# Attention and gated network on one core: stores of the folded weights put ahead in their queues, and other banks for the first transposes

## Chip, core and metric

The kernel runs on one core of a Trainium2 chip. The metric is the device time of one execution in microseconds (us). TensorE (PE) multiplies, VectorE (DVE), ScalarE (ACT) and GpSimd (POOL) work elementwise, SyncE (SP) issues most of the DMAs. Each engine takes its own instructions in the order of its queue and waits on semaphores for those of others.

## What is computed

Four batches of eight heads, 768 positions, 64 columns a head: attention over a window of 15 positions to each side and over 24 block summaries (the maximum of the keys and the mean of the values of each block of 32). The result, 3072 tokens by 512, goes through a gated network.

```python
k_sum = k.reshape(B, H, nb, block, D).max(axis=3)
v_sum = v.reshape(B, H, nb, block, D).mean(axis=3)
scores_all = concat([where(mask_l, scale * q @ k.T, -1e9), scale * q @ k_sum.T + log(block)])
a = softmax(scores_all)
x = (a @ concat([v, v_sum])).transpose(0, 2, 1, 3).reshape(B * S, H * D)
a = x @ w1
b = x @ w2
out = (a * b @ w3) @ w_out
```

## The kernel before

**Folding.** `w3 @ w_out` is multiplied once, at the start, into eight tiles `wp0` to `wp7` of 128 by 512 (in the trace's order their names are wp_80 to wp_87). Every weight arrives in halves as raw words (`wraw`), is rebuilt on ACT (L167) and DVE (L175, L178), cast on ACT into a high part (L188) and subtracted on DVE into a low part (L109). Products take three passes: high by high, low by high, high by low. `fold_weights` (from L193) accumulates tile i over j = 0 to 7 in one PSUM bank. When j = 7 is done, `store` (L209) empties the bank: a cast on ACT (L211, `wp`), and a subtraction on DVE (L109, `wp`) that needs the cast. The bank is free only after both.

**Banks.** PSUM has eight. Two carry the tag `mm` (products of the network, and fold tiles 0, 1 and 4 to 7), two the tag `tp` (transposes, the attention's output `po`, and the fold tiles 2 and 3, by `SIDE` = 4, L199), four the tag `sc` (scores, and the product of the means). A tile takes the next bank of its tag in turn.

**Attention in steps.** A step s is a pair of heads for 512 tokens. On PE it has scores (`sc`, L319, 32 small matmuls), transposes of the softmax (`tp`, L373, 16) and the product with the values (`po`, L393, 32). In between, DVE subtracts the maximum (L333, eight), ACT takes exponentials (L347, eight, each with its sum), POOL and DVE invert the sum (L352, L353), and ACT normalises (L362, eight; in step 0 it is one DVE instruction, L364). ACT copies the transposes out (L378 and L380 or, by `SECOND`, DVE for the second); after `po` ACT casts and DVE subtracts into `x` (L404, L109).

**Order.** PE and SP run in the order written. In the first stage the loop over `t` (L641) interleaves the fold, the conversions of weights and the first eight steps (`first_pair`, L555), which begin at the times of `FIRST`. ACT, DVE and POOL are ordered by a scheduler's priorities, which follow the order of the program; `tc.high_priority(offset=SOONER)`, with 400, moves instructions ahead of up to that much earlier work. The network's own evacuations have it already (L434, L437, L456). Later stages take two steps at a time, with the second step's transposes in `sc` banks.

Of the kernel before, what the change touches and what calls it, by code (L numbers as in the profile page):

```python
# [48 lines left out]
SECOND = "AAAVAVVA"  # L49
SOONER = 400  # L50
# [20 lines left out]
def attention_moe(ctx, tc, qG, kW, kT, vP, vW, vB, mask, w1, w2, w3T, wo, out):  # L71
    nc = tc.nc
# [33 lines left out]
    wp = [const.tile([P, 2, DO], F32R, name=f"wp{i}") for i in range(NF)]  # L106

    def low(eng, dst, src, hi):
        eng.tensor_tensor(dst, src, hi.bitcast(F32), ALU.subtract)  # L109

    def products(acc, terms, first, last):
        for i, (a, b) in enumerate(terms):
            nc.tensor.matmul(acc, lhsT=a, rhs=b, start=first and i == 0, stop=last and i == len(terms) - 1)  # L113
# [79 lines left out]
    def fold_weights(order):  # L193
        acc = {}
        for i, j in order:
            while not {("w3", i, j * P // PIECE), ("wo", j // 2, j % 2 * DO // PIECE)} <= have:
                yield 0
            if j == 0:
                acc[i] = ps.tile([P, 512], F32, name="mm", tag="tp" if 2 <= i < SIDE else "mm", bufs=2)  # L199
            a, b = weights["w3", i][:, :, j], weights["wo", j // 2][:, :, j % 2]  # L200
            products(
                acc[i][:, :DO],
                [(a[:, 0], b[:, 0]), (a[:, 1], b[:, 0]), (a[:, 0], b[:, 1])],
                j == 0,
                j == NJ - 1,
            )
            yield 3 * DO

            def store(i=i):  # L209
                done = acc.pop(i)[:, :DO]  # L210
                nc.scalar.copy(wp[i][:, 0], done)  # L211
                low(nc.vector, wp[i][:, 1], done, wp[i][:, 0])

            if j == NJ - 1:
                later(store)
# [112 lines left out]
    def reduce(u, h, sc, sm, mx):  # L328

        for i in ORDER:  # L330
            blk = (u * NBLK + i) % BLOCKS
            j = h * NBLK + i
            nc.vector.tensor_tensor_reduce(  # L333
                out=sm[:, j],
                in0=sc[h][:, i * KR : (i + 1) * KR],
                in1=mask_sb[:, 0 if blk == 0 else 2 if blk == BLOCKS - 1 else 1],
                op0=ALU.add,
                op1=ALU.min,
                scale=-SCALE,
                scalar=3.0e38,  # L340
                accum_out=mx[:, 0, j : j + 1],
            )

    def expose(h, sm, mx):
        for i in ORDER:
            j = h * NBLK + i
            nc.scalar.activation(  # L347
                sm[:, j], sm[:, j], AF.Exp, bias=mx[:, 0, j : j + 1], scale=-1.0, accum_out=mx[:, 1, j : j + 1]
            )

    def invert(mx):
        nc.gpsimd.tensor_scalar(out=mx[:, 1], in0=mx[:, 1], scalar1=1e-9, scalar2=None, op0=ALU.add)  # L352
        nc.vector.reciprocal(mx[:, 2], mx[:, 1])  # L353

    def normalize(sm, mx):
        nc.gpsimd.tensor_tensor(sm, sm, mx[:, 2].unsqueeze(2).broadcast_to([P, NI, KR]), ALU.mult)  # L356

    def normalize_alone(s, sm, mx):

        if NORMALIZE[s] == "A":  # L360
            for j in range(NI):
                nc.scalar.activation(sm[:, j], sm[:, j], AF.Copy, scale=mx[:, 2, j : j + 1])  # L362
        else:
            nc.vector.tensor_tensor(sm, sm, mx[:, 2].unsqueeze(2).broadcast_to([P, NI, KR]), ALU.mult)  # L364

    def transposes(sm, **more):

        tp = [ps.tile([P, 512], F32, name="tp", **more or {"bufs": 2}) for _ in range(2)]
        for j in range(NI):
            for g in range(2):  # L370
                rows = slice(64 * g, 64 * g + 64)
                to, p = tp[g][:KR, j * 64 : j * 64 + 64], sm[rows, j]
                nc.tensor.transpose(to, p, ident[rows, rows])  # L373
        return tp

    def evacuate(tp, second="V"):
        pt = [sb.tile([KR, U], F32, name="pt", bufs=6) for _ in range(2)]
        nc.scalar.copy(pt[0], tp[0][:KR, :U])  # L378
        if second == "A":
            nc.scalar.copy(pt[1], tp[1][:KR, :U])  # L380
        else:
            nc.vector.tensor_copy(pt[1], tp[1][:KR, :U])  # L382
        return pt

    def outputs(pt, v):

        po = ps.tile([P, 512], F32, name="po", tag="tp", bufs=2)
        for i in range(NBLK):
            for g in range(2):
                at = (2 * i + g) * 64  # L390
                for h in range(2):
                    cols = slice(h * D, (h + 1) * D)
                    nc.tensor.matmul(  # L393
                        po[cols, at : at + 64],
                        lhsT=v[:, g, i, cols],
                        rhs=pt[g][:, (h * NBLK + i) * 64 : (h * NBLK + i + 1) * 64],
                        start=True,
                        stop=True,
                    )
        return po  # L400

    def keep_x(po, x):
        t = sb.tile([P, 2, U], F32R, name="x", bufs=6)
        nc.scalar.copy(t[:, 0], po[:, :U])  # L404
        low(nc.vector, t[:, 1], po[:, :U], t[:, 0])
        x.append(t)
# [99 lines left out]
    def place(s):  # L506
        return divmod(s, NPAIR)

    inputs, values, sms = {}, {}, {}

    def fetch(s):
        if s < NS:
            inputs[s] = load_scores(*place(s))

    def fetch_values(s):
        if s < NS:
            values[s] = load_values(*place(s))

    def fetch_sums(s):
        if s < NS:  # L520
            load_sums(*place(s), values[s])

    def fill(s):
        if s < NS:
            gather(*place(s), inputs[s][1])

    def begin(s):
        u, p = place(s)
        sm = sb.tile([P, NI, KR], F32, name="sm", tag="wf", bufs=5)
        mx = aligned([P, 3, NI], name="mx", bufs=4)  # L530
        sms[s] = sm, mx
        return u, sm, mx, scores(*inputs.pop(s))
# [14 lines left out]
    def prepare(s):  # L547
        for work, raw in loaded.pop(s, ()):
            work(raw)
        for load_, work in coming.pop(s, ()):  # L550
            loaded.setdefault(s + 1, []).append((work, load_()))
# [3 lines left out]
    def first_pair(s):  # L555

        u, sm, mx, sc = begin(s)
        yield
        reduce(u, 0, sc, sm, mx)
        reduce(u, 1, sc, sm, mx)  # L560
        expose(0, sm, mx)
        yield
        expose(1, sm, mx)
        invert(mx)
        yield
        normalize_alone(s, sm, mx)
        while t[0] < (FIRST + (FIRST[-1] + 5,))[s + 1]:
            yield
        pt = evacuate(transposes(sms.pop(s)[0]), SECOND[s])
        yield  # L570
        keep_x(outputs(pt, values.pop(s)), xs[u])

# [2 lines left out]
    def later(work):  # L575
        delayed.append([1, work])
# [106 lines left out]
    with tc.manual_schedule(engines={engines.PE}):  # L683
        for s in range(NFIRST, NS + 1, 2):
            now = (s, s + 1) if s < NS else ()
            last = (s - 2, s - 1) if s > NFIRST else ()
            for p in (s, s + 1):
                prepare(p)
                if s == NFIRST:
                    fetch(p)  # L690
                    fill(p)
                    fetch_values(p)
                    fetch_sums(p)
            for p in (s + 2, s + 3):
                fetch(p)
                fetch_values(p)
                fetch_sums(p)
            with tc.manual_schedule(engines={engines.Activation, engines.DVE}):
                spare = ({}, {"tag": "sc", "bufs": 4})
                tps = [transposes(sms.pop(p)[0], **more) for p, more in zip(last, spare)]  # L700
                pts = [evacuate(tp) for tp in tps]
                begun_now = [begin(p) for p in now]
                for p, pt in zip(last, pts):
                    keep_x(outputs(pt, values.pop(p)), xs[place(p)[0]])
                for u, sm, mx, sc in begun_now:
                    for h in range(2):
                        reduce(u, h, sc, sm, mx)
                        expose(h, sm, mx)
                    invert(mx)
                    normalize(sm, mx)  # L710
            for p in (s + 2, s + 3):
                fill(p)

            n = s + 2 - NFIRST
            m = NPAIR + 0.15
            run(ALL_FOLD + UNIT * (1 + (n / m if n <= m else 1 + (n - m) / NPAIR)))
        run(float("inf"))
# [57 lines left out]
```

## Time and profile before

| | us |
|---|---|
| median of three runs | 540.87 (540.83 to 541.28) |
| the profiled execution | 540.83 |
| its span in the trace | 539.0 |
| PE busy | 517.9 (96%) |
| DVE busy, ACT busy | 237.5, 238.9 (44% each) |
| POOL busy | 56.3 (10%) |

The profiled execution is 1.8 us longer than its span. Shares of the whole span hide that the first 130 us, with folding, conversion of weights and attention at once, are full on all engines, and that the rest is almost PE alone. In 40 slices of 13.5 us:

```profile
PE   2897999999999999999999999999999999999997
PEclk9988899999999999999999999999999999999999
DMA  8999689956524005544032141050160020000001
```

### The profile page before, as it was taken

How to read it: one execution, taken by the hardware profiler on the slowest of the kernel's cores; microseconds unless marked ns; L12 is line 12 of the kernel's file. 1: busy time of each engine (PE TensorE's matmuls, PEld its weight loads, DVE VectorE, ACT ScalarE, POOL GpSimd, SP SyncE). 2: the span in 40 equal slices, each digit the busy share in tenths (PEclk: the TensorE clock that was granted, in tenths of full speed). 3: DMA queues.
4: the chain of work that ended last, by engine and by line, in shares of the span. 5: the costliest groups of instructions: out<-in, count | busy, mean ns of one | idle time of the engine just before them, and what ended most of it. 6: DMA issues, size and time to landing. Idle time of an engine off the chain costs nothing.

```text
span 539.0 us, 9912 instructions
## 1 busy us (share of the span) xinstructions
PE 517.9 (96%) x3852; PEld 421.8 (78%) x3852; DVE 237.5 (44%) x686; ACT 238.9 (44%) x688; POOL 56.3 (10%) x103
## 2 busy tenths in 40 slices
PE   2897999999999999999999999999999999999997
PEld 1655777888788888888888888888888888888885
DVE  5868889999503226724244033252042351122210
ACT  5547898887345225226235144253162261222210
POOL 1001221111001101103003002011021020000000
PEclk9988899999999999999999999999999999999999
DMA  8999689956524005544032141050160020000001
GB/s 309 403 348 350 189 270 369 280 183 197 167 96 154 0 1 169 162 128 135 0 111 60 40 152 58 0 157 33 40 190 1 1 75 39 21 21 0 1 19 58
DMA packets 30574, 67.21 MB, mean 125 GB/s; under 512 B 4032, under 2 KB 7616, under 8 KB 30528
## 3 DMA queue, kind: packets, MB, share of 16 engines
q1 hardware_dynamic: 27072, 60.30, 35.2%
q10 hardware_dynamic: 3456, 6.29, 3.1%
q8 instruction: 30, 0.49, 0.4%
q14 instruction: 16, 0.13, 0.1%
HBM read 58.51 MB, written 6.29 MB: 120 GB/s over the span
## 4 chain that ended last, share of the span: by engine, by line
PE 91%; DVE 3%; ACT 3%; DMA 1%; issue 1%; POOL 0%; SPq 0%; POOLq 0%; ACTq 0%
PE mm L113 79%; PE po L393 5%; PE sc L319 4%; PE tp L373 2%; DVE w L109 1%; DMA wraw<-in_w3T_dram 1%; DVE wf L178 1%; ACT w L188 1%; PE means L260 1%; ACT sm L347 1%; DVE wf L175 1%; ACT wf L167 0%; ACT wp L211 0%; DVE wp L109 0%; POOL k L306 0%
## 5 line engine op out<-in xcount | busy, mean ns | idle before, releaser
L113 PE MATMUL mm<-x,w 128*128 128x512 f32 x1152 | 264.9, 390 | 0.0
L113 PEld LDWEIGHTS mm<-x,w 128*128 128x128 f32 x1152 | 215.4, 188 | 45.6 <-issue 0.5
L113 PE MATMUL mm<-wp,h 128*128 128x512 f32 x576 | 133.9, 391 | 0.0
L113 PEld LDWEIGHTS mm<-wp,h 128*128 128x128 f32 x576 | 107.5, 188 | 22.7 <-issue 0.2
L347 ACT ACTIVATE sm<-sm,mx 128x120 f32<-128x120 f32 x192 | 73.6, 387 | 19.9 <-DVE mx L333 19.9
L438 DVE TENSOR_TENSOR g<-mm,g 128x512 f32<-128x512 f32 x48 | 33.1, 689 | 90.6 <-PE mm L113 88.7
L439 ACT CAST h<-g 128x512 fp32r<-128x512 f32 x48 | 29.6, 618 | 87.7 <-DVE g L438 87.7
L113 PE MATMUL mm<-w,w 128*128 128x512 f32 x192 | 54.1, 435 | 12.6 <-ACT w L188 11.5
L113 PEld LDWEIGHTS mm<-w,w 128*128 128x128 f32 x192 | 38.2, 206 | 25.6 <-ACT w L188 13.3
L457 ACT COPY o<-mm 128x512 f32<-128x512 f32 x24 | 14.1, 585 | 81.3 <-PE mm L113 81.3
L109 DVE TENSOR_TENSOR h<-g,h 128x512 fp32r<-128x512 f32 x48 | 35.7, 743 | 24.2 <-ACT h L439 24.0
L435 ACT COPY g<-mm 128x512 f32<-128x512 f32 x48 | 28.0, 584 | 35.6 <-PE mm L113 35.2
L333 DVE CUSTOM_DVE_ANT_0 sm<-sc,mask_sb 128x120 f32<-128x120 f32 x192 | 41.0, 275 | 5.5 <-PE sc L319 5.5
L382 DVE COPY pt<-tp 120x512 f32<-120x512 f32 x19 | 12.4, 686 | 67.7 <-PE tp L373 67.7
L306 POOL COPY k<-ks 128x96 f32<-128x96 f32 (+1 forms) x32 | 10.1, 327 | 252.3 <-DMA k<-in_kW_dram 210.0
L347 ACT ACTIVATION_READ_ACCUMULATOR sm<-sm,mx 128x1 f32 x192 | 36.5, 190 | 0.0
L109 DVE TENSOR_TENSOR x<-po,x 128x512 fp32r<-128x512 f32 x24 | 16.6, 690 | 42.2 <-ACT x L404 42.2
L356 POOL TENSOR_TENSOR sm<-sm,mx 128x960 f32<-128x960 f32 x16 | 29.1, 1820 | 6.0 <-DVE mx L353 5.0
L167 ACT ACTIVATE wf<-wraw 128x512 f32<-128x512 f32 x40 | 26.1, 669 | 6.2 <-DMA wraw<-in_wo_dram 2.7
L188 ACT CAST w<-wf 128x1024 fp32r<-128x1024 f32 (+1 forms) x25 | 21.9, 875 | 12.8 <-DVE wf L178 12.7
L393 PEld LDWEIGHTS po<-pt,v 120*64 120x64 f32 x768 | 23.8, 138 | 4.7 <-issue 2.9
L109 DVE TENSOR_TENSOR w<-wf,w 128x1024 fp32r<-128x1024 f32 (+1 forms) x25 | 25.4, 1014 | 4.4 <-ACT w L188 4.1
(33 smaller groups left out, 281.1 us busy)
## 6 DMA issues: line engine op xcount, KB each, us to landing
k<-in_kW_dram SPq DMA_DIRECT2D x24, 368.0 KB
wraw<-in_w3T_dram SPq DMA_DIRECT2D x16, 512.0 KB
wraw<-in_w_dram SPq DMA_DIRECT2D x16, 512.0 KB
q<-in_qG_dram SPq DMA_DIRECT2D x24, 256.0 KB
raw<-in_kT_dram SPq DMA_DIRECT2D x16, 384.0 KB
out_dram<-o ACTq DMA_DIRECT2D x24, 256.0 KB
v<-in_vW_dram SPq DMA_DIRECT2D x24, 192.0 KB
raw<-in_vB_dram SPq DMA_DIRECT2D x12, 384.0 KB
```

What stands on the lines that cost most here:

```text
L109: eng.tensor_tensor(dst, src, hi.bitcast(F32), ALU.subtract)
L113: nc.tensor.matmul(acc, lhsT=a, rhs=b, start=first and i == 0, stop=last and i == len(terms) - 1)
L167: nc.scalar.activation(f[:, k * PIECE : (k + 1) * PIECE], words[:, :, 1].bitcast(F32), AF.Prelu, scale=2.0**-112, alpha=-(2.0**32),)
L188: nc.scalar.copy(hi, f)
L319: nc.tensor.matmul(sc[h][64 * g : 64 * g + 64, i * KR : (i + 1) * KR], lhsT=q[rows, i * P + 64 * g : i * P + 64 * g + 64], rhs=k[rows, i, ...
L333: nc.vector.tensor_tensor_reduce(out=sm[:, j], in0=sc[h][:, i * KR : (i + 1) * KR], in1=mask_sb[:, 0 if blk == 0 else 2 if blk == BLOCKS - ...
L347: nc.scalar.activation(sm[:, j], sm[:, j], AF.Exp, bias=mx[:, 0, j : j + 1], scale=-1.0, accum_out=mx[:, 1, j : j + 1])
L356: nc.gpsimd.tensor_tensor(sm, sm, mx[:, 2].unsqueeze(2).broadcast_to([P, NI, KR]), ALU.mult)
L393: nc.tensor.matmul(po[cols, at : at + 64], lhsT=v[:, g, i, cols], rhs=pt[g][:, (h * NBLK + i) * 64 : (h * NBLK + i + 1) * 64], start=True, ...
L435: nc.scalar.copy(g, a[:, :U])
L438: nc.vector.tensor_tensor(g, acc[1][:, :U], g, ALU.mult)
L439: nc.scalar.copy(h[:, 0], g)
```

## The change

The two instructions of `store` are issued with the priority that the network's evacuations have. The first step's transposes (s = 0) take two banks of the tag `sc`; the other seven steps of the first stage keep `tp`. `SPARE` is now a name used in both stages. The number and kind of instructions stay the same.

```diff
             def store(i=i):
                 done = acc.pop(i)[:, :DO]
-                nc.scalar.copy(wp[i][:, 0], done)
-                low(nc.vector, wp[i][:, 1], done, wp[i][:, 0])
+                with tc.high_priority(offset=SOONER):
+                    nc.scalar.copy(wp[i][:, 0], done)
+                    low(nc.vector, wp[i][:, 1], done, wp[i][:, 0])
...
+    SPARE = {"tag": "sc", "bufs": 4}
...
-        pt = evacuate(transposes(sms.pop(s)[0]), SECOND[s])
+        pt = evacuate(transposes(sms.pop(s)[0], **({} if s else SPARE)), SECOND[s])
...
-                spare = ({}, {"tag": "sc", "bufs": 4})
-                tps = [transposes(sms.pop(p)[0], **more) for p, more in zip(last, spare)]
+                tps = [transposes(sms.pop(p)[0], **more) for p, more in zip(last, ({}, SPARE))]
```

PE's order is the same in both. Line numbers after the change are one to three higher. On ACT, at the first step's exponentials (`sm,mx<-sm,mx`) and the first four stores, there stood:

```order
L347 ACTIVATE sm,mx<-sm,mx 128x120 x4
L211 CAST wp_80<-mm 128x512
L167 ACTIVATE wf<-wraw 128x512
L211 CAST wp_81<-mm 128x512
L347 ACTIVATE sm,mx<-sm,mx 128x120
L167 ACTIVATE wf<-wraw 128x512
L347 ACTIVATE sm,mx<-sm,mx 128x120 x3
L211 CAST wp_82<-mm 128x512
L188 CAST w_415<-wf 128x1024
L167 ACTIVATE wf<-wraw 128x512
L211 CAST wp_83<-mm 128x512
```

and there stands now:

```order
L348 ACTIVATE sm,mx<-sm,mx 128x120 x3
L212 CAST wp_80<-mm 128x512
L348 ACTIVATE sm,mx<-sm,mx 128x120
L167 ACTIVATE wf<-wraw 128x512
L212 CAST wp_81<-mm 128x512
L348 ACTIVATE sm,mx<-sm,mx 128x120
L167 ACTIVATE wf<-wraw 128x512
L212 CAST wp_82<-mm 128x512
L348 ACTIVATE sm,mx<-sm,mx 128x120 x2
L212 CAST wp_83<-mm 128x512
L348 ACTIVATE sm,mx<-sm,mx 128x120
```

All four stores stand ahead of the first step's last exponential, the last two of which followed it.

On DVE, at the first step's reciprocal and normalisation, there stood:

```order
L178 SCALAR_TENSOR_TENSOR wf<-wraw,wf 128x512 x2
L353 RECIPROCAL mx<-mx 128x8
L364 TENSOR_TENSOR sm<-sm,mx 128x960
L109 TENSOR_TENSOR wp_82<-mm,wp_82 128x512
L109 TENSOR_TENSOR w_415<-wf,w_415 128x1024
L109 TENSOR_TENSOR wp_83<-mm,wp_83 128x512
```

and there stands now:

```order
L178 SCALAR_TENSOR_TENSOR wf<-wraw,wf 128x512 x2
L109 TENSOR_TENSOR wp_82<-mm,wp_82 128x512
L109 TENSOR_TENSOR wp_83<-mm,wp_83 128x512
L354 RECIPROCAL mx<-mx 128x8
L365 TENSOR_TENSOR sm<-sm,mx 128x960
L109 TENSOR_TENSOR w_415<-wf,w_415 128x1024
```

The two subtractions of the stores have gone from behind the normalisation to ahead of it.

The third place is the store of fold tile 4 (wp_84), which lies between step 0's `x` and the reduction of step 2's scores (`ISA`). The weight w_666 is converted for fold tile 6. ACT and DVE had:

```order
L167 ACTIVATE wf<-wraw 128x512
L188 CAST w_666<-wf 128x1024
L404 CAST x<-po 128x512
L362 ACTIVATE sm<-sm,mx 128x120 x4
L211 CAST wp_84<-mm 128x512
L362 ACTIVATE sm<-sm,mx 128x120 x4
L167 ACTIVATE wf<-wraw 128x512 x2
...
L230 TENSOR_REDUCE ks<-raw 128x24 x2
L109 TENSOR_TENSOR x<-po,x 128x512
L109 TENSOR_TENSOR w_666<-wf,w_666 128x1024
L109 TENSOR_TENSOR wp_84<-mm,wp_84 128x512
L333 ISA sm,mx<-sc,mask_sb 128x120
```

and have now:

```order
L167 ACTIVATE wf<-wraw 128x512
L407 CAST x<-po 128x512
L363 ACTIVATE sm<-sm,mx 128x120 x4
L212 CAST wp_84<-mm 128x512
L363 ACTIVATE sm<-sm,mx 128x120 x4
L188 CAST w_666<-wf 128x1024
L167 ACTIVATE wf<-wraw 128x512 x2
...
L109 TENSOR_TENSOR x<-po,x 128x512
L231 TENSOR_REDUCE ks<-raw 128x24 x2
L109 TENSOR_TENSOR wp_84<-mm,wp_84 128x512
L109 TENSOR_TENSOR w_666<-wf,w_666 128x1024
L334 ISA sm,mx<-sc,mask_sb 128x120
```

The cast of w_666 has moved behind the store of wp_84 and all of step 1's normalisation, its subtraction behind that of wp_84, and the two reductions of keys (`ks`) behind the subtraction of `x`.

## Rows read from the trace of the kernel before

**Rows 1.** The page's busy times: us, share of the span, instructions.

```profile
PE 517.9 (96%) x3852; PEld 421.8 (78%) x3852; DVE 237.5 (44%) x686; ACT 238.9 (44%) x688; POOL 56.3 (10%) x103
```

**Rows 2.** Timeline of PE: start, duration, line, operation, tiles, count, idle time before and releaser.

```profile
41.40 5.73 PE L113 MATMUL mm<-w,w 128*128 128x512 f32 x24
49.54 0.27 PE L373 MATMUL tp<-ident,sm 64*120 64x64 f32 x1 [2.41 <-DVE wp L109]
51.27 1.10 PE L373 MATMUL tp<-ident,sm 64*120 64x64 f32 x15 [1.47 <-DVE wp L109]
52.31 1.88 PE L319 MATMUL sc<-k,q 64*64 64x120 f32 x32
54.11 4.87 PE L113 MATMUL mm<-w,w 128*128 128x512 f32 x15
58.92 1.15 PE L393 MATMUL po<-pt,v 120*64 120x64 f32 x32
...
62.73 1.05 PE L319 MATMUL sc<-k,q 64*64 64x120 f32 x32 [0.40 <-POOL k L306]
...
70.24 1.15 PE L393 MATMUL po<-pt,v 120*64 120x64 f32 x32
...
78.86 1.15 PE L393 MATMUL po<-pt,v 120*64 120x64 f32 x32
...
87.81 1.15 PE L393 MATMUL po<-pt,v 120*64 120x64 f32 x32 [0.52 <-ACT pt L378]
```

**Rows 3.** Timeline of ACT, POOL and DVE around the first step's normalisation.

```profile
46.65 0.39 ACT L347 ACTIVATE sm<-sm,mx 128x120 f32<-128x120 f32 x1
...
47.22 0.24 POOL L352 TENSOR_SCALAR mx<-mx 128x8 f32<-128x8 f32 x1 [4.49 <-ACT sm L347]
...
47.73 1.16 DVE L364 TENSOR_TENSOR sm<-sm,mx 128x960 f32<-128x960 f32 x1
...
50.53 0.68 DVE L109 TENSOR_TENSOR wp<-mm,wp 128x512 fp32r<-128x512 f32 x1
```

**Rows 4.** Stretches: us, busy by engine, granted PE clock (PEclk, 0.50 is half), DMA share, GB/s.

```profile
29.34:32.76 3.42, 3.42 (x10) 2.64 (x9) 2.73 (x6) 1.34 (x3) 0.59 (x1) 0.50 1.06 355
49.82:56.65 6.83, 5.38 (x53) 4.47 (x54) 6.76 (x24) 4.79 (x15) 0.00 (x0) 0.50 0.86 289
...
46.41:49.82 3.41, 0.98 (x5) 0.39 (x3) 3.01 (x6) 3.41 (x9) 0.24 (x1) 1.00 1.07 240
```

**Rows 5.** Timeline of ACT from the store of fold tile 4 on.

```profile
62.37 0.59 ACT L211 CAST wp<-mm 128x512 fp32r<-128x512 f32 x1 [0.52 <-PE mm L113]
62.85 1.25 ACT L362 ACTIVATE sm<-sm,mx 128x120 f32<-128x120 f32 x4
64.01 1.22 ACT L167 ACTIVATE wf<-wraw 128x512 f32<-128x512 f32 x2
65.12 0.39 ACT L347 ACTIVATE sm<-sm,mx 128x120 f32<-128x120 f32 x1
...
68.61 0.60 ACT L380 COPY pt<-tp 120x512 f32<-120x512 f32 x1
...
78.02 0.58 ACT L380 COPY pt<-tp 120x512 f32<-120x512 f32 x1
...
81.75 1.05 ACT L188 CAST w<-wf 128x1024 fp32r<-128x1024 f32 x1
```

**Rows 6.** Timeline of DVE between step 0's output and step 2's scores.

```profile
58.37 1.76 DVE L230 TENSOR_REDUCE ks<-raw 128x24 f32<-128x768 f32 x2
...
61.34 1.22 DVE L109 TENSOR_TENSOR w<-wf,w 128x1024 fp32r<-128x1024 f32 x1
...
63.84 0.28 DVE L333 CUSTOM_DVE_ANT_0 sm<-sc,mask_sb 128x120 f32<-128x120 f32 x1 [0.16 <-PE sc L319]
```

**Rows 7.** Timeline of POOL: the copies of block maxima into the keys.

```profile
42.47 0.26 POOL L306 COPY k<-ks 128x96 f32<-128x96 f32 x1
...
61.53 1.36 POOL L306 COPY k<-ks 128x96 f32<-128x96 f32 x2
```

## The prediction

> **What bounds the kernel now.** I read the page first, then the chain of work that ended last, then PE's timeline where the chain leaves PE. PE is busy 96% of the span [rows 1], and from the first network product on the chain is PE's alone: a change in the first stage reaches the end only by moving PE's own work. PE's timeline has one large hole there. The fold's first four tiles end at 41.40 + 5.73 = 47.13; step 0's first transpose runs at 49.54, the other fifteen wait until 51.27, and both waits end with DVE's subtraction of a store (`wp`) [rows 2]. The two banks of `tp` still hold fold tiles 2 and 3, whose stores are queued late: the second's subtraction runs from 50.53 [rows 3]. The data of the transposes was there earlier: the normalisation ends at 47.73 + 1.16 = 48.89 [rows 3].
>
> The hole costs a second time through PE's clock. The granted clock was at its full level (2.4 GHz) until 49.82, in a stretch of 3.41 us of which PE worked 0.98, and then at half (1.2 GHz) until 56.65 [rows 4]. Fifteen fold products took 4.81 us there (54.11 to 58.92) [rows 2], while 24 took 5.73 at the full clock, 0.239 each. With 2.54 us of the 4.81 at half, 5.5 products fell in it: 0.46 each.
>
> **Part by part: the first step's transposes.** In `sc` banks they wait for the normalisation alone, but the normalisation is later, since all four stores now stand ahead of the last exponential on ACT and ahead of the reciprocal on DVE. From rows: fold tile 3 ends at 47.13; with about 0.05 from an end to the start that waits for it (51.21 to 51.27) [rows 2, 3] its cast begins at 47.18; the next ACT instruction follows 0.48 after a cast (62.37 to 62.85) [rows 5], so the last exponential starts at 47.66 instead of 46.65. POOL's sum follows 0.57 later, DVE's normalisation 0.51 after that, and it lasts 1.16 [rows 3]: it ends at 49.90. DVE's subtraction of that store can start when the cast (0.59) is done, at 47.8, and with its 0.68 ends at 48.5, when the reciprocal becomes due (the normalisation starts at 48.74, the reciprocal about 0.25 ahead of it): it costs nothing, 0.1 if it is late. The transposes start at 49.95 and, with 16 x 0.069 = 1.11 us at half clock (fifteen took 1.04), the scores of step 1 begin at 51.06 instead of 52.31: **1.25 us gained**. The waits of 2.41 and 1.47 become one of 2.8. No banks are short: step 1's scores take those that step 0's scores have left long before, and step 2's take the transposes' after their copies.
>
> **The clock.** 49.95 is after the moment at which the clock fell, so these transposes still run at half. Whether it comes back earlier than at 56.65 is the open question. If not, the scores (1.80 us) end at 52.86, 3.79 us at half do 8.3 products and 6.7 x 0.239 = 1.60 follow: `po` of step 0 starts at 58.25 instead of 58.92, and **0.58 of the 1.25 is given back**. The other half-clock stretch of this trace lasted 3.42 us, from 29.34 on, with PE busy all through [rows 4]. If this one ends after as long, at 53.24, then 0.39 us do 0.8 products, 14.2 follow in 3.38, and `po` starts at 56.62, a gain of 2.30. For it: PE would now be busy from 49.95 to 53.24 as it was there. Against it: these 3.3 us are nearly all transposes and scores of 64 rows, where the stretch that came back had products of 128 by 512. I take the late return, at 3 to 2.
>
> **The keys of step 2.** Its scores wait 0.40 for POOL's copy of the maxima [rows 2], the first of two that took 1.36, beside the subtraction at 61.34 [rows 6, 7]. Now the reductions of the keys come behind `x`, where that subtraction stood: the first ends at 61.34 + 0.88 = 62.22. If the copy then takes 0.26, as alone [rows 7], the scores start near 62.55 instead of 62.73 (all on before's time of PE): **0.1 to 0.2 gained, I take 0.1**. If the copy also waits for the second reduction (63.1), 0.7 is lost.
>
> The Trainium skill, "SBUF — State Buffer", section "Who interferes with whom", has GpSimd held up by a DVE instruction with two SBUF inputs and never by a reduction. The 1.36 beside a two-input subtraction agrees, and a copy beside a reduction is in no row here; by the page the gain of 0.1 stands.
>
> **The conversion of w_666.** Here the change adds a wait. Before, its cast ran on ACT at a time when ACT then idled for step 0's `po`, so it was free. Now it follows the store of tile 4 and four normalisations, which end at 64.01 [rows 5]; the cast lasts 1.05 [rows 5], the subtraction 1.22 [rows 6], and the reduction of step 2's scores is queued behind that subtraction on DVE. It starts at 64.01 + 1.05 + 1.22 less overlap = 66.25 instead of 63.84 [rows 6], and the first exponential, about 0.38 after (0.28 and the read of the minimum), at 66.63 instead of 65.12: ACT is **1.5 us late** from here, 0.95 by the cast and the rest waiting for DVE. Behind the exponentials are queued the copies of the transposes, and PE waits for those. In step 1 the second copy ends at 68.61 + 0.60 = 69.21 and PE takes `po` at 70.24: a cover of 1.03. In step 2 it is 78.60 against 78.86: 0.26 [rows 2, 5]. ACT has no idle time between, so the 1.5 us come out as about 0.45 of waiting at the first and 0.7 at the second, **1.15 lost** (1.5 less 0.26, less 0.1 of slack). Ends: nothing, if the queues have slack that the merged rows hide; 1.5 if the cover is thinner.
>
> **Step 3.** Its `po` already waits 0.52 for ACT [rows 2], behind a cast that needs DVE's words; on DVE the subtraction of step 2's `x` now comes ahead of a reduction, which makes those words later. Between 0 and 0.5 again; **I take 0.3 lost**.
>
> **The rest.** Stores 5 to 7 move by an instruction or two, and the banks that they free are wanted a whole fold tile later: nothing. On SP one load of values moves ahead of two weight loads late in the stage; the reductions that free its buffer move ahead on DVE too, the weights are converted long after they land, and in the trace before no later wait of PE is for a weight: nothing, at worst 1 us.
>
> **Sum**: -1.25 + 0.58 - 0.1 + 1.15 + 0.3 = +0.7. The profiled execution, 540.83 (span 539.0), is the median of 540.87 to 0.04, so the forecast is **541.5**, which is within 0.2% (1.1 us), about the least that a measurement here tells from no change. Its own range is 540.8 to 542.3.
>
> **Rivals.**
> The clock returns at 53.24: -2.30 - 0.1 + 1.15 + 0.3 = -0.95, 539.9. For and against as above. Chance 0.30.
> The queues absorb the conversion of w_666: the gain of the transposes stays, 540.1 with the late clock and 538.5 with the early one. For it: the ACT queue re-orders only by one cast. Against: between the store of tile 4 and the copies of step 2 ACT has next to no idle time to give. Chance 0.10.
> The clock does not fall at all, since PE resumes sooner than at 49.82: at twice the speed 0.56 of transposes, 0.9 of scores and 3.6 of products bring `po` to 55.0, 3.9 earlier, of which the later waits for POOL and ACT take back about 2; some 539. Against: the chain of waits above is closed by data, not by queues. Chance 0.05.
> Slower: the lateness of ACT and DVE does not end with step 3. The mechanism is the reduction of step 2's scores, stuck behind w_666's subtraction, and after it the weights of the last gates, whose conversion goes through the same two queues. It decides when the lateness left at step 3 is over the 0.5 that PE waits there now; each later `po` can then cost another 0.4 to 0.7, and the copy for step 2's keys 0.7: 542.3 to 543. For it: both engines are busy almost all the time there. Against: PE waited for neither between step 3 and the last steps. Chance 0.12.
> The change not doing what it says (the transposes still waiting for a store) is excluded by the order: only the normalisation is left ahead of them.
>
> **How the numbers follow.** The forecast has 0.43. Its own spread of 0.7 puts a quarter of it beyond 541.95, so slower is 0.11 from it and 0.11 from the slow rival: 0.22. Faster by over 0.2% (below 539.8) is 0.12 of the early clock, 0.06 of the absorbed queues and 0.05 of the clock that stays: 0.23. Same is 0.55. The range for eight in ten leaves out the fast ends and the worst of the slow rival: 539.2 to 542.5.
>
> **What would show it.** Right: in the profile after, one wait of 2.7 to 2.9 us ahead of step 0's transposes, ended by DVE's L365 (L364 before); scores of step 1 about 1.3 us earlier; new waits of PE for ACT's copies ahead of `po` in steps 1 and 2, together about 1.1. Wrong: transposes starting before 49.8, a granted clock of 1.0 at 54, PE not waiting ahead of `po` in step 2, or a wait for weights after the first gate.

## The result, and the profile after

The changed kernel takes 541.9 us (median of 20 runs, 538.9 to 545.4) where the kernel before takes 540.1 in the runs beside it (20 runs, 538.4 to 541.6). The ratio is 1.0037, with a 95% interval from 1.0023 to 1.0051: slower by about 2.0 us. The time lies inside the range that was given, but not in the case that was called likeliest: of the cases, "slower by over 0.2%" came true, and the forecast of +0.7 was too small. Three executions that took 865, 587 and 2913 us (of the kernel before, of e6 and of e8) are left out of every median and difference below.

The profiled execution after takes 541.11 with a span of 539.3. Its page shows PE with less work time than in [rows 1], although it takes longer, and a new number in the costliest group, 1.3 us of idle time ahead of products of the gates:

```profile
PE 515.5 (96%) x3852; PEld 419.8 (78%) x3852; DVE 237.6 (44%) x686; ACT 239.2 (44%) x688; POOL 56.6 (10%) x103
...
L113 PE MATMUL mm<-x,w 128*128 128x512 f32 x1152 | 265.1, 390 | 1.3 <-DVE g L441 1.3
```

PE's timeline after (columns as in [rows 2]), from the fold's first four tiles to the last gate:

```profile
39.82 5.73 PE L113 MATMUL mm<-w,w 128*128 128x512 f32 x24
48.46 1.11 PE L376 MATMUL tp<-ident,sm 64*120 64x64 f32 x16 [2.91 <-DVE sm L365]
49.49 1.88 PE L320 MATMUL sc<-k,q 64*64 64x120 f32 x32
51.30 3.86 PE L113 MATMUL mm<-w,w 128*128 128x512 f32 x15
55.09 1.15 PE L396 MATMUL po<-pt,v 120*64 120x64 f32 x32
...
58.90 1.05 PE L320 MATMUL sc<-k,q 64*64 64x120 f32 x32 [0.39 <-POOL k L307]
...
66.41 1.49 PE L396 MATMUL po<-pt,v 120*64 120x64 f32 x32
...
75.78 1.51 PE L396 MATMUL po<-pt,v 120*64 120x64 f32 x32 [0.34 <-ACT pt L381]
...
85.51 1.15 PE L396 MATMUL po<-pt,v 120*64 120x64 f32 x32 [0.94 <-ACT pt L381]
86.59 13.92 PE L113 MATMUL mm<-x,w 128*128 128x512 f32 x60
...
123.14 0.34 PE L396 MATMUL po<-pt,v 120*64 120x64 f32 x4
124.06 1.24 PE L396 MATMUL po<-pt,v 120*64 120x64 f32 x28 [0.58 <-issue]
125.23 4.38 PE L113 MATMUL mm<-x,w 128*128 128x512 f32 x18
130.92 8.45 PE L113 MATMUL mm<-x,w 128*128 128x512 f32 x36 [1.32 <-DVE g L441]
139.21 3.11 PE L113 MATMUL mm<-wp,h 128*128 128x512 f32 x13
```

The reader is to see three things. The hole ahead of step 0's transposes is now one wait of 2.91 that ends with the normalisation, as worked out; the store no longer ends it. The `po` of steps 1, 2 and 3 carry new waits: 0.34 inside the first (1.49 long where [rows 2] has 1.15), 0.34 ahead of and 0.36 inside the second, 0.94 instead of 0.52 ahead of the third. And far behind, at 123 and 131, PE waits where the kernel before did not wait at all.

Two distances say how much each is worth. From step 0's `po` to the first gate product before took 29.97 us (58.92 to 88.89); after it is 31.50 (55.09 to 86.59). From there to the first product with `wp`, which stood at 138.95 before, it was 50.06; now it is 52.62. What follows is the same to 0.04 us. So 1.5 and 2.6 us are lost in two places, and only the first was in the prediction's sum.

The third piece, the hole and the clock, can't be read from this pair of profiles alone: the stretch at half clock near 29 us [rows 4], which cost before 1.6 us, is absent in this execution though nothing ahead of it was changed. The stretches after (columns as in [rows 4]) are:

```profile
28.39:32.36 3.97, 3.97 (x17) 3.26 (x18) 3.25 (x6) 1.20 (x2) 0.24 (x1) 1.00 1.04 390
44.82:48.23 3.41, 0.73 (x4) 0.27 (x2) 3.31 (x7) 3.41 (x11) 0.23 (x1) 1.00 1.07 304
48.23:51.64 3.41, 3.18 (x49) 2.79 (x50) 3.38 (x6) 2.26 (x5) 0.00 (x0) 0.50 1.02 290
```

The late loss is followed best from SP. Its timeline after, ahead of the last gates:

```profile
96.12 9.90 SPq L241 DMA_DIRECT2D raw<-in_vB_dram  x2
106.12 0.85 SPq L147 DMA_DIRECT2D wraw<-in_w_dram  x2
108.02 4.26 SPq L241 DMA_DIRECT2D raw<-in_vB_dram  x2
112.33 0.70 SPq L147 DMA_DIRECT2D wraw<-in_w_dram  x1
```

and the same queue before:

```profile
98.13 0.38 SPq L240 DMA_DIRECT2D raw<-in_vB_dram  x1
99.23 0.93 SPq L147 DMA_DIRECT2D wraw<-in_w_dram  x2
109.65 4.57 SPq L240 DMA_DIRECT2D raw<-in_vB_dram  x2
114.31 0.38 SPq L147 DMA_DIRECT2D wraw<-in_w_dram  x1
```

Blocks of keys and values of the later batches (`raw`) share two buffers. Of the value blocks of the third batch (`raw<-in_vB`) the first finds one free, the second stands for 9.2 us until DVE has reduced the block of keys that is in the other; in the kernel after it does so ahead of two weight loads, which leave at 106.12 instead of 99.23. (The part of this document on the kernel before says that SP runs in the order written. For the loads of the first stage among themselves that holds; these value blocks are emitted in the second stage and are put among them by the scheduler.) The last weight leaves at 112.33 after and at 114.31 before, which by itself is sooner; but it comes later to ACT, which waits longer for it. ACT's row before:

```profile
118.93 0.69 ACT L167 ACTIVATE wf<-wraw 128x512 f32<-128x512 f32 x1 [1.45 <-DMA wraw<-in_w_dram]
```

and its row after:

```profile
119.90 0.66 ACT L167 ACTIVATE wf<-wraw 128x512 f32<-128x512 f32 x1 [4.36 <-DMA wraw<-in_w_dram]
```

The chain of waits after, in order of time (start, us, what), goes through the same place:

```profile
112.33 7.54 DMA wraw<-in_w_dram
...
119.90 0.66 ACT wf L167
120.56 0.95 ACT w L188
...
127.87 0.95 ACT w L188
...
128.85 1.33 DVE w L109
130.18 0.61 DVE g L441
...
130.92 9.13 PE mm L113 x39
```

The last weight was under way for 7.54 us. Counted from the first gate product, ACT takes it up at 33.31 us (119.90 less 86.59) where before it was at 30.04 (118.93 less 88.89): 3.3 us later. Only 0.3 of this is a later issue (25.74 against 25.42 on SP); the other 2.95 pass between its issue and ACT's start (7.57 us against 4.62). The reason lies in what SP held back. The DMA engines had next to nothing to do while SP stood, and from 108 on they were full until the weight was there; before, they were not. The first two rows are of the kernel after, the third is of the kernel before (columns as in [rows 4], here PE, PEld, DVE, ACT, POOL):

```profile
102.00:106.00 4.00, 4.00 (x29) 3.04 (x27) 4.00 (x19) 4.00 (x14) 0.00 (x0) 1.00 0.02 6
108.00:120.00 12.00, 12.00 (x94) 9.73 (x93) 10.15 (x16) 7.26 (x18) 1.77 (x3) 1.00 0.99 270
109.60:119.00 9.40, 9.40 (x43) 7.74 (x43) 8.56 (x14) 7.61 (x20) 1.57 (x3) 1.00 0.59 179
```

So the last weight is late less because it waits on SP than because the loads that SP gave out late fill the DMA engines together with it. This is read from these rows; no run tells the two apart.

ACT stands 4.36 us for this one half of a weight; behind it wait the cast, the copies of the transposes and the gates' evacuations, then DVE, and PE at 130.92.

### The profile page after: what moved, and what is told of

The parts are those of the page before. It is cut to its first block, busy times and chain, and to the rows that moved or that the text cites. A ratio compares the mean times of both kernels' runs of the same rounds, so it can differ in the third digit from the quotient of the medians.

```text
span 539.3 us, 9916 instructions
## 1 busy us (share of the span) xinstructions
PE 515.5 (96%) x3852; PEld 419.8 (78%) x3852; DVE 237.6 (44%) x686; ACT 239.2 (44%) x688; POOL 56.6 (10%) x103
## 4 chain that ended last, share of the span: by engine, by line
PE 83%; ACT 8%; DVE 5%; DMA 2%; issue 1%; SPq 0%; ACTq 0%
PE mm L113 72%; PE po L396 4%; PE sc L320 4%; ACT sm L348 2%; PE tp L376 2%; DVE w L109 2%; ACT w L188 2%; ACT sm L363 1%; DMA wraw<-in_w_dram 1%; DVE wf L178 1%; DMA wraw<-in_w3T_dram 1%; PE means L261 1%; ACT wf L167 1%; DVE wf L175 1%; ACT wp L212 1%
## 5 line engine op out<-in xcount | busy, mean ns | idle before, releaser
L113 PE MATMUL mm<-w,w 128*128 128x512 f32 x192 | 50.8, 414 | 13.3 <-ACT w L188 12.2
L113 PEld LDWEIGHTS mm<-w,w 128*128 128x128 f32 x192 | 35.9, 194 | 25.3 <-ACT w L188 13.8
L396 PE MATMUL po<-pt,v 120*64 120x64 f32 x768 | 26.9, 225 | 2.3 <-ACT pt L381 1.5
```

The costliest lines, as they stand in the source:

```text
L396: nc.tensor.matmul(po[cols, at : at + 64], lhsT=v[:, g, i, cols], rhs=pt[g][:, (h * NBLK + i) * 64 : (h * NBLK + i + 1) * 64], start=True, ...
```

## Experiments

Three theories stood for the 4 us that were lost. **Theory 1**: the late loss comes from the value blocks ahead of weight loads on SP. **Theory 2**: the loss up to the first gate is w_666's conversion, which the change put behind the store of tile 4. **Rival** to both: ACT and DVE are simply full, and a PE that is sooner out of the hole waits for them later, whatever stands in the queues.

Since the half-clock stretches come and go between executions of one kernel (the mean granted clock of the kernel before lay between 0.987 and 0.997 of full), times are given in three ways: the median, the ratio to the kernel before, and the difference at the same clock. The last comes from all runs whose clock is on record: within a kernel the time rises by 0.32 us for each 0.001 that its mean granted clock is lower (one straight line for all kernels, standard error 0.02), and kernels are compared on that line. At the same clock the change costs 2.7 us (plus or minus 0.4). The gap to 2.0 is the clock: after ran at 0.994 on average, before at 0.992 (in the runs beside e1 to e10; of the 20 beside after no clock is on record). The distances A (step 0's `po` to first gate product) and B (from there to the first product with `wp`) come from each kernel's profile.

| kernel | median | ratio, 95% interval | at the same clock | A | B |
|---|---|---|---|---|---|
| before | 540.1 | | | 29.97 | 50.06 |
| after | 541.9 | 1.0037 [1.0023, 1.0051] | +2.7 | 31.50 | 52.62 |
| e2, stores alone | 541.15 | 1.0028 [1.0009, 1.0047] | +2.2 | 31.48 | 53.25 |
| e3, after, weights first | 540.02 | 1.0000 [0.9981, 1.0019] | +0.8 | 31.49 | 50.09 |
| e4, after, w_666 early | 539.40 | 0.9980 [0.9961, 0.9998] | +0.6 | 31.28 | 50.03 |
| e5, e3 and e4 together | 539.72 | 1.0001 [0.9985, 1.0017] | +0.4 | 31.33 | 49.98 |
| e6, before, weights first | 539.29 | 0.9995 [0.9978, 1.0012] | -0.2 | 29.98 | 50.00 |
| e7, e3 and w_666's cast on POOL | 539.19 | 0.9979 [0.9959, 0.9998] | -0.5 | 30.44 | 50.09 |
| e1, banks alone | 540.55 | 1.0017 [0.9999, 1.0035] | +2.4 | 32.04 | 51.69 |
| e8, banks alone, weights first | 538.36 | 0.9979 [0.9962, 0.9996] | 0.0 | 32.04 | 50.01 |
| e9, three stores, banks, both cures | 538.79 | 0.9996 [0.9970, 1.0021] | +0.8 | 32.65 | 50.03 |
| e10, banks, both cures | 538.97 | 0.9973 [0.9960, 0.9985] | +0.3 | 32.04 | 50.16 |

The kernel before had a median of 540.1 beside after, 539.6 beside e2 to e5, 539.7 beside e1 and e6 to e8, 540.2 beside e9 and e10. The differences at the same clock are uncertain by 0.5. They are least fair where an edit itself changes how long PE is at half clock (e1, e8, e9 and e10, whose hole is shorter); there the ratio counts.

**e2: the stores without the banks.** Step 0's transposes go back to the two `tp` banks.

```diff
-        pt = evacuate(transposes(sms.pop(s)[0], **({} if s else SPARE)), SECOND[s])
+        pt = evacuate(transposes(sms.pop(s)[0]), SECOND[s])
```

> The stores' part of the change alone: the queues of every engine stand as in the kernel after, only step 0's transposes lie in the two tp banks again. If the banks matter, the transposes wait for a store again and the time is up to 2 us above the kernel after (about 543.5). If the sooner stores alone have freed the banks before the normalisation ends, the transposes still start after one wait that ends with the normalisation, and the time is that of the kernel after, 541.9 against 540.1 before (ratio 1.003 to 1.004).

The transposes still wait 2.91 for the normalisation, and the time is that of the kernel after within the intervals. With the stores sooner the banks are worth nothing that these runs can tell. This profile has the same two half-clock stretches as the profile before (6.83 us the second), so it is the fair partner for [rows 2]:

```profile
40.73 1.05 PE L320 MATMUL sc<-k,q 64*64 64x120 f32 x32
50.40 1.11 PE L374 MATMUL tp<-ident,sm 64*120 64x64 f32 x16 [2.91 <-DVE sm L365]
...
58.59 1.15 PE L394 MATMUL po<-pt,v 120*64 120x64 f32 x32
```

From step 0's scores to its `po` it is 17.86 us. Before, with step 0's scores at 40.41 in the same timeline, it was 18.51: a gain of 0.65, where the sum had 1.25 less 0.58.

**e3: the weight loads first.** The first two value blocks of the third batch are loaded by the hand-written order of the first stage, after the last weight.

```diff
...
-            loaded.setdefault(s + 1, []).append((work, load_()))
+            loaded.setdefault(s + 1, []).append((work, ahead.pop(0) if ahead else load_()))
...
+    WORK[38] = [lambda: ahead.append(load_blocks(2, 0))]
...
-        46: [lambda: fetch_values(7), lambda: fetch_sums(7)],
+        46: [lambda: fetch_values(7), lambda: fetch_sums(7), lambda: ahead.append(load_blocks(2, 1))],
```

> The kernel after, with the loads of the third batch's value blocks queued on SP behind the last four weight loads; nothing ahead of about 95 us is moved. Theory 1 (the late loss is the last weights, which land late because a value-block load that waits for its buffer stands ahead of them on SP): the wait for the last weight on ACT (4.36 us) and PE's waits behind the gates between 123 and 132 us go, and 2.0 to 2.5 us come back: 539.4 to 539.9, at or below the kernel before. Rival (the late loss is what is left of ACT's and DVE's lateness from the conversion of w_666): the weights land sooner but the time stays at 541.6 to 541.9.

B falls from 52.62 to 50.09, ACT waits for no weight any more, and 1.9 us come back both in the medians and at the same clock (540.02 is 0.1 above the times that were expected). SP's timeline of this run has the four weight loads in one row:

```profile
98.03 4.49 SPq L147 DMA_DIRECT2D wraw<-in_w_dram  x4
108.65 0.34 SPq L241 DMA_DIRECT2D raw<-in_vB_dram  x1
```

A stays at 31.49, so the two losses are separate things: theory 1 holds for the late one, against the rival, which had A's lateness go on into the gates.

**e4: w_666's conversion sooner; e5: with the weights first as well.** All four kinds of instruction of that conversion get the stores' priority (the cast is shown).

```diff
-        nc.scalar.copy(hi, f)
+        with tc.high_priority(offset=SOONER) if (name, i) == ("w3", 6) else ExitStack():
+            nc.scalar.copy(hi, f)
```

> The kernel after, with the whole conversion of w_666 (the words, the shift, the cast and the subtraction) given the stores' priority: its cast stands ahead of step 0's x again, and with it SP's order is that of the kernel before. Theory 1 alone (weights): 539.4 to 539.9. Theory 2 on top (w_666 behind the store of tile 4 costs 1.1 to 1.4 us in waits of PE ahead of po in steps 1 to 3): 538.2 to 538.8, with those waits gone from the trace. If neither holds: 541.9.

> Both edits: w_666 converted early, and the value blocks of the third batch behind the last weight loads. By theory 1 and 2 together 538 to 538.8, at most 0.5 below the run with w_666 alone (whose last weight is still behind value blocks whose buffers come free late, as in the kernel before). If theory 1 is all there is, the same as the run with the weight loads first, 539.4 to 539.9.

In e4 SP's order is that of before, and B is 50.03: a second way to take the late loss away, by another edit. But theory 2 got no answer: A fell by 0.2 us alone. The cast does stand ahead of `x` now; in exchange the scheduler put three of step 1's exponentials behind `x` (three at 0.38 each), so about as much work of ACT came into the stretch as left it. And at the same clock e4 is within 0.2 us of e3. e5 came out with both of them (539.72, B 49.98): one cure is enough for the late loss, and the 538 to 538.8 of both theories together was missed.

**e6: the weights first in the kernel before.**

> The kernel before with the third batch's value blocks behind the last four weight loads, as in the run with the weight loads first. In the trace of before the last weight is waited for by ACT too (1.45 us at 118.93) but no product of PE waits for it. If the cost of theory 1 starts only when the lateness exceeds that cover: 540.1, ratio 0.999 to 1.001. If before pays for it as well: 0.5 to 1 us faster, ratio 0.998.

No change that can be told. The 1.45 us that ACT waits for a weight before are hidden. How much more is hidden follows from the four kernels without a cure, by the time from the first gate product to ACT's start on the last weight, and by B:

| | last weight, after the first gate product | later than before | B, more than before |
|---|---|---|---|
| before | 30.04 | | |
| e1 | 32.37 | 2.33 | 1.63 |
| after | 33.31 | 3.27 | 2.56 |
| e2 | 33.94 | 3.90 | 3.19 |

All three lose what the weight is late, less 0.70 or 0.71. That is the cover.

**e7: w_666's cast on POOL, on top of e3.**

```diff
-        nc.scalar.copy(hi, f)
+        (nc.gpsimd.tensor_copy if (name, i) == ("w3", 6) else nc.scalar.copy)(hi, f)
```

> The kernel after with the weight loads first, and with w_666's cast moved from ACT to POOL, where it comes after the copies of step 1's value sums: ACT's queue between step 0's x and the copies of step 2 is then that of before without any cast of a whole weight tile in it. Theory 2: from step 0's po to the first gate product PE takes 31.5 us with the cast on ACT (29.97 in before); without it 30.0 to 30.4, so the time is 1.1 to 1.5 us under that of the run with the weight loads first: 538.6 to 539. Rival (the lateness is ACT's and DVE's whole load at an earlier PE, whichever cast it is): still 31.2 or more, and the same time. A price that may show: POOL's copy of the keys' maxima for step 2 waits behind the cast, and PE's scores with it, up to 1 us.

Here ACT's queue keeps its order and only loses the cast. PE's timeline of this run:

```profile
69.58 1.15 PE L396 MATMUL po<-pt,v 120*64 120x64 f32 x32
...
78.20 1.15 PE L396 MATMUL po<-pt,v 120*64 120x64 f32 x32
...
87.52 1.15 PE L396 MATMUL po<-pt,v 120*64 120x64 f32 x32 [0.89 <-ACT pt L381]
88.60 6.66 PE L113 MATMUL mm<-x,w 128*128 128x512 f32 x28
```

The waits of steps 1 and 2 are gone, that of step 3 is left (0.89), and A is 30.44, that is 1.05 under e3. The two copies in ACT's queue show the same: step 2's second copy ends 0.25 ahead of its `po`, where before it was 0.26 [rows 2, 5]. ACT's row:

```profile
77.36 0.59 ACT L383 COPY pt<-tp 120x512 f32<-120x512 f32 x1
```

Theory 2 holds for steps 1 and 2, in the form that e4 and e7 leave of it: PE waits for the amount of work that stands on ACT behind step 0's `x`. In the kernel after the surplus is w_666's cast; three exponentials in its place (e4) cost nearly as much. POOL took 1.04 us for the cast, and its copy of the keys behind it made step 2's scores wait 0.48 instead of 0.37.

**e8 and e1: the banks without the stores,** with and without the weights first.

> The other part of the change alone, with the weight loads first: the kernel before with step 0's transposes in banks of sc, the stores at their old priority. The transposes then wait for the normalisation alone, which is not pushed back by the store of tile 3: they start about 1 us sooner after the fold than in the kernel after (1.9 us instead of 2.91). If the sooner transposes pay: 538.5 to 539.2. If ACT's and DVE's queues set PE's pace up to the first gate whatever the hole: the same as the run of the kernel after with the weight loads first, within 0.4 us.

> The banks alone, without the edit to the loads: SP's queue comes out as in the kernel after (two value blocks ahead of the last two weights of the next-to-last pair). Theory 1: 2.0 to 2.5 us above the same kernel with the weight loads first, 541 to 541.7. If the late loss needs the sooner stores: as fast as the kernel with the weight loads first.

The pair tells the weights again: 2.2 us in the medians, 1.7 in B (2.0 to 2.5 was expected; e1 itself, at 540.55, was faster than the 541 to 541.7 expected of it). With the banks alone SP's queue comes out as in the kernel after, so neither part of the change owns the late loss; the scheduler brings it with either. The hole is 1.9 us here, since the store of tile 3 is behind the last exponential, and PE is at half clock for a shorter time. But A is 32.04, the longest so far, and the reason stands in e8's timeline:

```profile
59.07 1.05 PE L319 MATMUL sc<-k,q 64*64 64x120 f32 x32 [1.49 <-POOL k L306]
...
85.12 1.15 PE L393 MATMUL po<-pt,v 120*64 120x64 f32 x32 [1.23 <-ACT pt L378]
```

Two microseconds of what the hole gave up are waited for again, for POOL's copy (itself waiting for DVE's reduction of the keys) and for ACT. To that extent the rival is right: a PE that is sooner out of the hole waits for the other engines up to the first gate.

**e9 and e10: versions from the findings.** e9 gives the priority to the stores of tiles 0 to 2 alone, e10 to none; both have the banks, the cast on POOL and the weights first.

> A version built from the findings: the banks of the change, the store's priority for tiles 0 to 2 alone (so the store of tile 3 stands behind the last exponential, as in before), w_666's cast on POOL, and the weight loads first. By the theories: the hole ahead of step 0's transposes is 1.9 us instead of 2.91 (or 3.9 in before), PE takes 30.4 from step 0's po to the first gate product as in the run with the cast on POOL, no loss between the gates: 537.8 to 538.8, ratio to before 0.996 to 0.998. Against: where the sooner transposes only make PE wait for ACT and POOL later, as in the run with the banks alone (1.49 us for the copy of the keys' maxima), 539.

> The banks alone with the weight loads first and w_666's cast on POOL, all stores at their old priority. Against the run without the cast on POOL it tells whether the cast still costs where exponentials of step 1 stand behind step 0's x: by theory 2 another 0.5 to 1 us less, 537.8 to 538.3. If the wait of step 2's scores for POOL (1.49 us) sets the pace, the cast on POOL adds to it and the time is the same or up to 0.5 us more.

e10 has the lowest ratio of the study: 0.9973, with all of its interval below 1, some 1.5 us under the kernel before. The ratios of e4, e7 and e8 (0.9979 and 0.9980) lie inside its interval, so it can't be called the best. The cast on POOL freed step 2's `po` there too (its row is back at 1.15), but the scores of step 2 wait 1.72 for POOL instead of 1.49, and A is what it was without it: e8 and e10 can't be told apart. e9's runs lie between 537.4 and 543.9 and tell nothing for certain; its profile, with no half-clock stretch but in its last microsecond, has the shortest span of all, 536.0, and again gives most of it back in A (1.95 us for POOL, 1.60 for ACT).

## Why the prediction was right or wrong

**The hole: right.** One wait of 2.91 (2.7 to 2.9 was given), ended by L365. The gain with the late clock was sized -0.67, and e2 against [rows 2] shows -0.65.

**The clock: right in both cases.** With the same hole the second half-clock stretch lasted 6.8 us in the profiles of e2, e3, e4, e5 and e7 (late), and 3.41 in that of after (early); 3 to 2 was given for the late one, and six profiles can't confirm odds. For the early case the sum had -2.30 up to `po`; after needs 16.25 us from step 0's scores (38.84 in its timeline) to `po` against 18.51, which is -2.26. What was missed is that before varies as well, in the stretch near 29 us, so that a single profile of either can't be compared to better than 1.6 us.

**The keys of step 2: wrong, by 0.1.** The wait is 0.39 where it was 0.40. The first reduction came where the prediction put it: it starts 2.43 behind the start of `po` (57.52 less 55.09), where the subtraction before started 2.42 behind. But it lasted 0.94 instead of 0.88, and the copy began 0.12 after its end, so step 2's scores start 3.81 behind `po` in both kernels. The copy itself took what was said, beside a reduction:

```profile
57.52 1.80 DVE L231 TENSOR_REDUCE ks<-raw 128x24 f32<-128x768 f32 x2
```

```profile
58.58 0.26 POOL L307 COPY k<-ks 128x96 f32<-128x96 f32 x1 [0.84 <-POOL v L295]
```

The first row is DVE's, the second POOL's, both of after. The 1.36 in [rows 7] is two copies; the first of them, beside the subtraction at 61.34, reads by itself:

```profile
61.53 1.15 POOL L306 COPY k<-ks 128x96 f32<-128x96 f32 x1
```

That a reduction doesn't hold GpSimd up is what the Trainium skill, "SBUF — State Buffer", section "Who interferes with whom", says; here the trace agrees, 0.26 beside a reduction against 1.15 beside a subtraction.

**The conversion of w_666: right.** 1.15 was given for steps 1 and 2; in after the waits are 0.34, 0.34 and 0.36, together 1.04, and e7 takes 1.05 away with the cast. **Step 3**: 0.3 was given, 0.42 measured (0.94 less 0.52).

**"The rest": wrong, and this is the step that failed.** It priced SP's reordering at "nothing, at worst 1 us", since "the weights are converted long after they land, and in the trace before no later wait of PE is for a weight". The second half is true and the first is not: ACT waits 1.45 us for the last weight in the trace before (the row stands above). The argument looked at PE's waits alone. A wait that is hidden from PE has a cover, and the cover is the thing to size: 0.7 us by e1, e2 and after, against two weights that leave 7 us later behind a load that waits for its buffer, and a last weight that reaches ACT 3.3 us later. The term should have read 2.6.

**The slow rival** named the place, "the weights of the last gates, whose conversion goes through the same two queues", and "a wait for weights after the first gate" stands among the signs of being wrong, but its cause was to be the lateness of ACT and DVE left at step 3. e3 has that lateness in full (A 31.49) and none of the late loss. So the rival's time came true (+2.0; 542.3 to 543 was given on 540.87) by another mechanism, which had no chance of its own in the prediction.

**The sum**, in its own terms: -0.65, 0 for the keys, +1.04, +0.4 and +2.6 make +3.4 with the late clock and +1.8 with the early one. The runs lie between, +2.0. That their median fell inside the range that was given is therefore in part luck: with the late clock, which was called the likelier, 540.83 and 3.4 make 544.2, outside of it. With the forecast's terms but the last it would have been +0.8 and -0.8; the forecast of +0.7 was right for the part of the program that it looked at (e3, the kernel after without the late loss, is at +0.8 at the same clock, though its ratio is 1.0000).

## What to carry to other kernels

When a change moves instructions, compare the order of every queue to its end, that of the DMA issues above all: a load that waits for a buffer holds up all loads behind it (here for 9.2 us), these then crowd the DMA engines together, and a scheduler may put it there for an edit elsewhere. For each load behind such a wait, look up the engine that consumes it and how much later it may come before another engine has to wait; a wait that is there already and costs nothing (here 1.45 us on ACT) is a sign that little is left. And where the kernel's runs scatter by more than the change is worth, compare two profiles only over stretches in which they had the same clock.

## What was not expected of the hardware

The half-clock stretch near 29 us, which is ahead of everything that was edited, is there in 5 of the 12 profiles (before, e1, e2, e7, e10) and absent in 7. Step 0's scores start at 40.35 to 40.73 us with it and at 38.63 to 39.05 without it. So the same untouched part of the program takes two times about 1.6 us apart, by nothing in its instructions that the profiles show. The stretch after the hole lasted 6.8 us in before and in e2 to e7, but 3.41 in after, whose hole is that of e2, e3, e4, e5 and e7; with a hole of 1.9 us it lasted 3.4 in e1, e8 and e10, and in e9, with 2.42, there was none. What decides its length stays open.
